# Two layers of linear attention and squared-ReLU feed-forward on one core: the second group's tiles by seven products per pair, M's differences on GpSimd

## The chip, the core and the metric

One core of one Trainium2 chip runs the whole program. The metric is the device time of one execution in microseconds (us), the median of three runs of the same kernel. A profile of one further execution gives the timing of every instruction. Its engines are called as the profile calls them: PE (TensorE matmuls), PEld (TensorE weight loads), DVE (VectorE), ACT (ScalarE), POOL (GpSimd) and SP (the queue that issues the DMAs).

## The reference, cut to what matters

```python
def _A_ref(x, wqkv, wo):                    # S = 2048, D = 640, 32 heads of 20
    q, k, v = split_heads(x @ wqkv)
    phi = lambda t: where(t > 0, t + 1, exp(t)) + 1e-6
    pq, pk = phi(q), phi(k)
    kv = einsum("bhsd,bhse->bhde", pk, v);  z = sum_s(pk)
    o = (pq @ kv) / (pq . z + 1e-6)
    return merge_heads(o) @ wo

def _B_ref(x, w1, b1, w2, b2):              # F = 1728
    h = relu(x @ w1 + b1)
    return (h * h) @ w2 + b2

x = x + A(layernorm(x));  x = x + B(layernorm(x))
x = x + A(layernorm(x));  x = x + B(layernorm(x))
```

Everything is float32. The kernel folds `kv` of all heads and `wo` into one matrix M of 640 x 640, so that the attention's output for a tile of 128 rows is `pT @ M`, where `pT` is the tile's normalized query features, transposed.

## The kernel before, in words

The 2048 rows are 16 tiles of 128 rows, and four groups of four tiles (`TG = 4`). Every float32 operand of a matmul is split in a high part (written by ACT, rounded for TensorE) and a low part (DVE: the value less its high part), and a product is three matmuls, high by low, low by high and high by high (`mm3`, L399 to L403). Matrices M are five row blocks `M[0]` to `M[4]` of 128 rows, each split so.

Each of the two layers has three stages.

**Stage A** (L712 to L841) goes once over the 16 tiles: layer norm, the projections to k and q, their feature maps (`Phi`, L495: `exp` on ACT at L501, then `rest` with DVE's L508 and L509, which empties the PSUM bank), and the sums over rows that M is made of. POOL adds up the key features (`acc`, L697).

**The passage** (L844 to L1052) finishes the q parts that were left over (`late_q`, L847, three PSUM banks in turn from L1043 on: 1, 2, 3), makes M (`kv_make`, `m_make` into the raw rows `m_raw`, L979, L935 to L952; `m_split` writes the split M, L954), and brings the first group's four tiles to the feed-forward stage. For tiles 0 to 3 that is: product with M (`proj`, L424), the residual sum (`b_x1`, L668), the layer norm (`b_norm`, L671: `ln_stats`, L355, with two bn_stats and bn_aggr on DVE and then an add at L362 and a power at L363 on POOL; `ln_apply`, L368, on DVE), and the transposition, by 32 x 32 blocks for tiles 0 and 1 (`blocks_T`, L378, on DVE, then sixteen block moves on ACT, L391) and by TensorE for tiles 2 and 3 (`f_trans`, L1006 and L372). All engines take their instructions in the order in which the program writes them, so `late_q` parts fill PE between these steps. A new `late_q` part may begin in its bank only when L509 has read that bank's earlier part.

**The feed-forward stage** (L1583 to L1615) loops over four groups g and, in each, over 14 blocks c of F. A step is `fc1` (15 matmuls, L1083), `act` (ACT's Relu at L1094, DVE's L1095 to L1097 make the split h), and `fc2` of the block before (15 matmuls, L1132). Between the matmul groups of a step, `run(g, c, place)` calls what a table `events` has for that place: the attention tiles of the **next** group are worked in there. For groups 2 and 3 they go in pairs (`side`, L1491; `Pair`, L1348): two tiles share seven products of half width (320 columns) with sums and differences of row blocks, `p1` to `p7`, of 18 block products together. The needed differences of M's blocks, `ta` and `tb`, are made once per layer by `m_turns` (L1279) on DVE and ACT, out of the split M, at steps 6 to 13 of group 0 (`TURN0`, L67). For group 1 (tiles 4 to 7), worked in during group 0, each tile goes by itself (`single`, L1453): ten half-width block products per tile (two halves of five), at steps 3, 5, 8 and 10 (`OUT0`, L66).

Weights of the feed-forward blocks come through a ring of six buffers by SP (L310). In the first layer two blocks of `w1` and `w2` that stay in memory are loaded raw into the space of `x1` (`raw_stay`, L321, called from L1250) and split in group 0 (`split_stay`, L329).

At the very start PE does `N_WARM` transposes of the identity (L547 to L549) while the first loads are under way.

Of the kernel before, what the change touches and what calls it, by code (L numbers as in the profile page):

```python
# [8 lines left out]
F32 = mybir.dt.float32  # L9
# [29 lines left out]
N_WARM = 25  # L39
# [13 lines left out]
def fast(b):  # L53
    return pair_plan(
        b, (b - 3, 0), (b - 2, 0), [(b - 1, 0), (b - 1, 1), (b - 1, 2), (b - 1, 3)],
        {"p1": (b, 0), "p4": (b, 1), "p6": (b, 2), "p7": (b, 3), "p5": (b, 4),
         "p2": (b + 1, 0), "p3": (b + 1, 2)},
        [((b, "post"), (b + 1, 0), (b + 1, 1), (b + 2, 0), (b + 2, 1), (b + 2, 3)),
         ((b + 1, 3), (b + 1, "post"), (b + 2, 0), (b + 2, 4), (b + 3, 0), (b + 3, 1))],
    )  # L60
# [5 lines left out]
OUT0 = (3, 5, 8, 10)  # L66
TURN0 = (  # L67
    [(6, 2), (7, 2), (7, 3), (8, 1), (8, 2), (8, 3), (8, 4)],
    [(9, 2), (10, 2), (10, 3), (11, 1), (12, 3), (13, 2), (13, 3)],
)  # L70
# [8 lines left out]
def kernel(  # L79
# [50 lines left out]
    def ftile(name):  # L130
        return tmp.tile([P, D], F32, tag="f", name=name, bufs=F_BUFS)
# [223 lines left out]
    def ln_stats(t, xt):  # L355
        st = small.tile([P, 2, 6], F32, tag="bn", name="bn")
        for j in range(2):
            nc.vector.bn_stats(st[:, j], xt[:, j * HD : (j + 1) * HD])
        mv = small.tile([P, 2], F32, tag="mv", name="mv")
        nc.vector.bn_aggr(mv, st)  # L360
        rs = small.tile([P, 1], F32, tag="rs", name="rs")
        nc.gpsimd.tensor_scalar(rs, mv[:, 1:2], LN_EPS, None, op0=ALU.add)  # L362
        nc.gpsimd.tensor_tensor(out=rs, in0=rs, in1=neghalf, op=ALU.pow)  # L363
        sts[t] = mv, rs
# [78 lines left out]
    def a_stats(t):  # L443
        if t < NT:
            ln_stats(("a", t), xt[t])
# [12 lines left out]
    for layer in range(N_LAYERS):  # L458
# [82 lines left out]
        if layer == 0:  # L541
# [11 lines left out]
            a_stats(0)  # L553
# [399 lines left out]

        def m_split(m):  # L954
# [54 lines left out]

        po = {}  # L1010
# [41 lines left out]
        late_rest()  # L1052
        sa.close()
# [200 lines left out]
        def stay(c):  # L1254
# [7 lines left out]

        ta, tb, so = wtile("uT13"), wtile("uT42"), wtile("uS")
        ta, tb, so = (
            ta.rearrange("p (j m n) -> p j m n", j=2, m=2),
            tb.rearrange("p (j m n) -> p j m n", j=2, m=2),
            so.rearrange("p (j n) -> p j n", j=2),
        )  # L1270

        def m_whole(m):
            v = ftile("mf")
            nc.vector.tensor_tensor(
                out=v, in0=M[m][:, 0].bitcast(F32), in1=M[m][:, 1].bitcast(F32), op=ALU.add
            )
            return v

        def m_turns(m):  # L1279

            b1 = m_whole(m)
            yield
            b2 = m_whole(m + 2)
            lo, hi = slice(0, HD), slice(HD, D)
            for i, (out, x, y) in enumerate((
                (b1[:, lo], b1[:, hi], b1[:, lo]),
                (b1[:, hi], b2[:, hi], b1[:, hi]),
                (b2[:, hi], b2[:, hi], b1[:, lo]),
                (b2[:, lo], b2[:, lo], b2[:, hi]),
            )):  # L1290
                if i % 2 == 0:
                    yield
                nc.vector.tensor_tensor(out=out, in0=x, in1=y, op=ALU.subtract)
            yield
            for u, v in ((ta, b1), (tb, b2)):
                nc.scalar.activation(u[:, 0, m], v, AF.Copy)
            for u, v in ((ta, b1), (tb, b2)):
                yield
                nc.vector.tensor_tensor(
                    out=u[:, 1, m], in0=v, in1=u[:, 0, m].bitcast(F32), op=ALU.subtract  # L1300
                )

# [150 lines left out]
        def single(i, b, d, at):  # L1453

            t = TG + i
            if i > 0:
                at(d - 3, "post", lambda: b_load_pq(t))
            at(d - 1, "post", lambda: b_den(t))
            at(d, "post", lambda: b_blocks(t))
            s = d + (i == 0)  # L1460
            at(s, "post", lambda: blocks_move(yzp[t], (0, 1)))
            at(s + 1, "pre", lambda: blocks_move(yzp[t], (2, 3)))
            steps(at, lambda: p_split(t), *[(d + 2, "pre") if i == 0 else (d + 1, "post")] * 2)
            at(b - 3, "post", lambda: b_load_x(t))
            ps = []

            def out():
                yzp.pop(t)
                for j in range(2):
                    s = slice(j * HD, (j + 1) * HD)  # L1470
                    ps.append(fresh(f"po{j}")[:, :HD])
                    for c in range(DC):
                        a = pT[t][:, :, c * P : (c + 1) * P]
                        mm3(ps[j], a[:, 0], a[:, 1], M[c][:, 0, s], M[c][:, 1, s], c == 0, c == DC - 1)
                pT.pop(t)

            def add():
                for j in range(2):
                    v = xr[t][:, j * HD : (j + 1) * HD]
                    nc.vector.tensor_tensor(out=v, in0=ps[j], in1=v, op=ALU.add)  # L1480
                ln_stats(("b", t), xr[t])
                norm(t)

            at(b, "pe", out)
            at(b + 1, "pre", add)
            at(b + 1, "post", lambda: blocks_move(yzx[t], (0, 1)))
            at(b + 1 + 3 * (i == 3), "post", lambda: f_bias(t))
            at(b + 2, "pre", lambda: blocks_move(yzx[t], (2, 3)))
            steps(at, lambda: x_split(t), (b + 2, "post"), (b + 2, "post"))

        def side(g, p, plan, at):  # L1491

            t0, t1 = TG * g + 2 * p, TG * g + 2 * p + 1
            m0, m1, turn, out, back = plan["moves0"], plan["moves1"], plan["turn"], plan["out"], plan["back"]
            for t, (s, pl) in ((t0, m0), (t1, m1)):
# [7 lines left out]
            steps(at, lambda: p_split(t0), (m0[0] + 1, 0), (m0[0] + 1, 2))  # L1503
# [13 lines left out]
            for t, (st, ap_, (s, pl), hi, lo, bi) in ((t1, back[0]), (t0, back[1])):  # L1517
                at(*st, lambda t=t: ln_stats(("b", t), xr[t]))
                at(*ap_, lambda t=t: norm(t))
                for k in range(4):  # L1520
                    at(s + (pl + k) // 5, (pl + k) % 5, lambda t=t, k=k: blocks_move(yzx[t], (k,)))
# [5 lines left out]
        for g in range(NG - 1):  # L1527
# [3 lines left out]
            for p in range(TG // 2):  # L1531
# [5 lines left out]
                if g > 0:  # L1537
                    side(g + 1, p, OUTS[p], at)
            if g == 0:
                for i, b in enumerate(OUT0):  # L1540
                    single(i, b, OUT0[i - 1] if i else 1, at)

                for m in range(2):
                    steps(at, lambda m=m: m_turns(m), *TURN0[m])

# [38 lines left out]
        for g in range(NG):  # L1584
            for c in range(NF):
# [62 lines left out]
```

## Time and profile before

| | |
|---|---|
| time, median of three runs (lowest, highest) | 1345.11 us (1344.97, 1345.32) |
| the profiled execution's own time | 1345.5 us |
| its span, first to last instruction | 1343.4 us |
| what lies around the span | 2.1 us |
| instructions | 19038 |

A row of a group names the line, the engine, the operation, what is written and read, and how often; then the busy time. A row of the timeline is start, duration, engine, line, operation, tiles and count; in brackets stands the idle time of the engine just before, and what ended it. A row of the chain of work that ended last is start, duration, engine and line. A row of a table by stretches has the stretch, its length and each engine's busy time in it.

### The profile page before, as it was taken

To read this page: it belongs to the slowest core of one execution; us is meant where nothing else is said; L and a number is where in the kernel's file an instruction comes from. 1 tells how busy PE (TensorE), PEld (TensorE's weight loads), DVE (VectorE), ACT (ScalarE), POOL (GpSimd) and SP (SyncE) were. 2 spreads that over 40 slices of the span, in tenths; PEclk is the share of its full clock that TensorE was granted. 3 is DMA by queue.
4 is the path that set the end of the run, shared out by engine and by line. 5 is a ranking of instruction groups with operands and counts; after the bars stand their busy time and mean duration, and the time that the engine had idled before them with its cause. 6 is when DMAs were issued, how large, how long until landed. Compare 5 with 4: busy or idle time off the path is not lost.

```text
span 1343.4 us, 19038 instructions
## 1 busy us (share of the span) xinstructions
PE 1337.6 (100%) x6773; PEld 1156.1 (86%) x6773; DVE 924.0 (69%) x1670; ACT 787.3 (59%) x1992; POOL 123.3 (9%) x172
## 2 busy tenths in 40 slices
PE   9999999999999999999999999999999999999998
PEld 8888999988888888888888899998888888888887
DVE  8888868777776776643467678677678667766323
ACT  5888848676547448512647686494746466474120
POOL 2222210000000000000012232100000000000000
PEclk9999999999999999999999999999999999999999
DMA  6787825574645565487521115156546456555635
GB/s 206 255 298 272 286 91 179 197 272 150 245 163 176 201 250 173 156 311 276 221 98 50 49 40 156 41 206 258 178 152 244 167 182 230 196 173 176 248 130 193
DMA packets 85635, 253.43 MB, mean 189 GB/s; under 512 B 11030, under 2 KB 19606, under 8 KB 84902
## 3 DMA queue, kind: packets, MB, share of 16 engines
q1 hardware_dynamic: 85398, 252.04, 53.6%
q8 instruction: 53, 0.87, 0.3%
q14 instruction: 40, 0.33, 0.1%
q10 hardware_dynamic: 144, 0.20, 0.0%
HBM read 193.50 MB, written 56.03 MB: 186 GB/s over the span
## 4 chain that ended last, share of the span: by engine, by line
PE 99%; DMA 0%; ACT 0%; SPq 0%; DVE 0%; DVEq 0%; issue 0%
PE PS L403 38%; PE PS L1132 28%; PE PS L1083 28%; PE PS L424 3%; PE PS L927 1%; PE PS L940 1%; PE PS L736 1%; DMA st<-in_A_wqkv_dram 0%; PE PS L372 0%; PE PS L877 0%; PE PS L1172 0%; ACT kq L189 0%; DVE x L1183 0%; SPq L211 0%; SPq L441 0%; DVEq L1643 0%
## 5 line engine op out<-in xcount | busy, mean ns | idle before, releaser
L391 ACT ACTIVATE z<-y 32x160 f32<-32x160 f32 x1392 | 465.1, 334 | 75.2 <-DVE y L378 59.1
L1083 PE MATMUL PS<-xTb,u 128*128 128x512 f32 x1400 | 333.1, 389 | 0.0
L1083 PEld LDWEIGHTS PS<-xTb,u 128*128 128x128 f32 x1400 | 262.0, 188 | 54.4 <-ACT hr L1094 0.8
L403 PE MATMUL PS<-kq,xT 128*128 128x320 f32 (+2 forms) x1575 | 284.3, 334 | 0.0
L1132 PE MATMUL PS<-u,h 128*128 128x512 f32 x1120 | 276.7, 390 | 0.0
L403 PEld LDWEIGHTS PS<-kq,xT 128*128 128x128 f32 x1575 | 250.3, 188 | 27.3 <-DVE rl L509 1.0
L1132 PEld LDWEIGHTS PS<-u,h 128*128 128x128 f32 x1120 | 208.5, 188 | 40.8
L1094 ACT ACTIVATE hr<-PS,b1sb 128x512 f32<-128x512 f32 x104 | 71.5, 687 | 277.3 <-PE PS L1083 276.4
L1095 DVE TENSOR_TENSOR hr<-hr 128x512 f32<-128x512 f32 x104 | 71.7, 690 | 219.7 <-ACT hr L1094 219.2
L403 PE MATMUL PS<-kh,xh 128*128 128x512 f32 x480 | 124.1, 392 | 0.0
L501 ACT ACTIVATE e<-PS 128x320 f32<-128x320 f32 (+4 forms) x128 | 53.6, 436 | 107.2 <-PE PS L403 98.7
L362 POOL TENSOR_SCALAR rs<-mv 128x1 f32<-128x1 f32 x64 | 28.0, 438 | 865.4 <-DVE mv L360 865.4
L403 PEld LDWEIGHTS PS<-kh,xh 128*128 128x128 f32 x480 | 87.1, 188 | 15.2 <-DVE kh L700 0.4
L508 DVE TENSOR_SCALAR e<-e 128x320 f32<-128x320 f32 (+4 forms) x128 | 41.6, 325 | 69.9 <-ACT e L501 69.4
L1132 PE MATMUL PS<-h,u 128*128 128x512 f32 x280 | 79.0, 390 | 0.0
L1097 DVE TENSOR_TENSOR h<-hr,h 128x512 fp32r<-128x512 f32 x104 | 72.0, 693 | 3.6
L697 POOL TENSOR_TENSOR acc<-acc,r 128x640 f32<-128x640 f32 x30 | 53.8, 1795 | 197.8 <-DVE r L509 197.8
L403 PE MATMUL PS<-uM,pT 128*128 128x320 f32 x408 | 66.2, 309 | 0.0
L403 PEld LDWEIGHTS PS<-uM,pT 128*128 128x128 f32 x408 | 62.3, 188 | 1.9
L1132 PEld LDWEIGHTS PS<-h,u 128*128 128x128 f32 x280 | 52.2, 188 | 10.8 <-DVE h L1108 0.4
L1083 PE MATMUL PS<-xTb,uw 128*128 128x512 f32 x240 | 57.0, 389 | 0.0
L509 DVE SCALAR_TENSOR_TENSOR r<-PS,e 128x512 f32<-128x512 f32 (+2 forms) x104 | 51.1, 492 | 6.1 <-ACT e L501 2.2
(135 smaller groups left out, 1458.5 us busy)
## 6 DMA issues: line engine op xcount, KB each, us to landing
u<-kept_w SPq DMA_DIRECT2D x184, 640.0 KB, 4.2
x<-x SPq DMA_DIRECT2D x48, 320.0 KB, 4.6
kept_w<-uprep SPq DMA_DIRECT2D x23, 640.0 KB, 4.6
pqt<-pq SPq DMA_DIRECT2D x32, 320.0 KB, 4.9
x<-xr SPq DMA_DIRECT2D x32, 320.0 KB, 3.8
st<-in_B_w_dram SPq DMA_DIRECT2D x22, 320.0 KB, 6.2
pq<-r SPq DMA_DIRECT2D x20, 320.0 KB
kept_kq<-kq SPq DMA_DIRECT2D x10, 640.0 KB, 6.2
```

Source lines behind the costliest of these rows:

```text
L391: nc.scalar.activation(d, v, AF.Copy)
L403: nc.tensor.matmul(ps, a, b, start=first and i == 0, stop=last and i == 2)
L424: nc.tensor.matmul(ps[:, j * 512 : j * 512 + HD], aT[:, k, c, :], w[c][:, l, j * HD : (j + 1) * HD], start=c == 0 and i == 0, stop=c == DC ...
L501: nc.scalar.activation(self.e[:, a:b], ps, AF.Exp)
L508: nc.vector.tensor_scalar(e, e, 1.0, PHI_EPS, op0=ALU.min, op1=ALU.add)
L509: nc.vector.scalar_tensor_tensor(out=self.r[:, a:b], in0=ps, scalar=0.0, in1=e, op0=ALU.max, op1=ALU.add)
L697: nc.gpsimd.tensor_tensor(out=acc, in0=acc, in1=r, op=ALU.add)
L1083: nc.tensor.matmul(ps, a[:, d, :], bb[:, d, :], start=n == 0, stop=n == len(order) - 1)
L1094: nc.scalar.activation(r, ps, AF.Relu, bias=b1sb[:, c : c + 1])
L1095: nc.vector.tensor_tensor(out=r, in0=r, in1=r, op=ALU.mult)
L1097: nc.vector.tensor_tensor(out=h[:, 1], in0=r, in1=h[:, 0].bitcast(F32), op=ALU.subtract)
L1132: nc.tensor.matmul(ps, l, r, start=first and k == 0, stop=last and k == len(a) - 1)
```

## The change

- `OUT0` becomes two pair plans. Group 1's four tiles go through `side` and `Pair` like those of groups 2 and 3, at steps 5 and 10 of group 0, the second pair with its block moves at steps 5 and 8 and one of its four groups of moves on DVE. `single`, `TURN0`, `m_whole` and `m_turns` go.
- `ta` and `tb` are made in the passage. `m_sums` takes the differences in place on the raw rows `m_raw` with POOL, four subtractions of half a row block for each of two m; `b_norm` issues two of them each time, behind `ln_stats` and ahead of `ln_apply`; what is left would come at the end (`m_sum(9)`). Then four splits (ACT and DVE) stand at the end of the passage, behind the last `late_rest` and ahead of the release of that stage's memory.
- In the pair plans, the high and low parts of the first tile's `x_split`, its `f_bias` and the low part of its `p_split` are put at other places.
- `split_stay` is called once at step 0 of group 0 in place of three times.
- 22 warm-up transposes in place of 25; the very first layer norm's epsilon is added by DVE in place of POOL.

```diff
-N_WARM = 25
+N_WARM = 22
-def fast(b):
+def fast(b, m0=None, m1=None):
     return pair_plan(
-        b, (b - 3, 0), (b - 2, 0), ...
+        b, m0 or (b - 3, 0), m1 or (b - 2, 0), ...
-         ((b + 1, 3), (b + 1, "post"), (b + 2, 0), (b + 2, 4), (b + 3, 0), (b + 3, 1))],
+         ((b + 1, 3), (b + 1, "post"), (b + 2, 0), (b + 2, "post"), (b + 3, "pre"), (b + 3, 4))],
-OUT0 = (3, 5, 8, 10)
-TURN0 = (
...
+OUT0 = (fast(5), {**fast(10, (5, 0), (8, 0)), "vec": ((0, 2),)})
+STAY = 1

-    def ln_stats(t, xt):
+    def ln_stats(t, xt, add=nc.gpsimd):
...
-        nc.gpsimd.tensor_scalar(rs, mv[:, 1:2], LN_EPS, None, op0=ALU.add)
+        add.tensor_scalar(rs, mv[:, 1:2], LN_EPS, None, op0=ALU.add)
         nc.gpsimd.tensor_tensor(out=rs, in0=rs, in1=neghalf, op=ALU.pow)
-            a_stats(0)
+            a_stats(0, add=nc.vector)

         def b_norm(t):
             ln_stats(("b", t), xr[t])
+            m_sum(2)
             xn[t] = ftile("xn")
             ln_apply(("b", t), xn[t], xr[t])

+        def m_sums(m):
+            b1, b2, lo, hi = m_raw[m], m_raw[m + 2], slice(0, HD), slice(HD, D)
+            for out, x, y in (
+                (b1[:, lo], b1[:, hi], b1[:, lo]),
+                (b1[:, hi], b2[:, hi], b1[:, hi]),
+                (b2[:, hi], b2[:, hi], b1[:, lo]),
+                (b2[:, lo], b2[:, lo], b2[:, hi]),
+            ):
+                nc.gpsimd.tensor_tensor(out=out, in0=x, in1=y, op=ALU.subtract)
+                yield
+        m_fill.extend(m_sums(m) for m in range(2))
...
         late_rest()
+        ta, tb, so = wtile("uT13"), wtile("uT42"), wtile("uS")
...
+        m_sum(9)
+        for u, v in ((ta, 0), (tb, 2)):
+            for m in range(2):
+                split(u[:, 0, m], u[:, 1, m], m_raw[m + v])
         sa.close()
...
-        def m_whole(m):
...
-        def m_turns(m):
...
-        def single(i, b, d, at):
...
-            steps(at, lambda: p_split(t0), (m0[0] + 1, 0), (m0[0] + 1, 2))
+            steps(at, lambda: p_split(t0), (m0[0] + 1, 0), (m0[0] + 1, 4))
...
-                    for _ in range(3 if c == 0 else 1):
+                    for _ in range(STAY if c == 0 else 1):
                         wu.split_stay()
```

More of the change, by code (lines that the diff above doesn't have):

```diff
@@ L1260, in stay @@
                 n_stage += 1
[L1265 to L1270, printed above, removed]
-        def m_whole(m):
[L1273 to L1277, printed above, removed]
-        def m_turns(m):
[L1281 to L1301, printed above, removed]
         def s_turns(t):
@@ L1451, in norm @@
             yzx[t] = blocks_T(xn.pop(t))
-        def single(i, b, d, at):
[L1455 to L1489, printed above, removed]
         def side(g, p, plan, at):
@@ L1535, in at @@
                     events.setdefault((*divmod(n, NF), place), []).append(f)
[L1537 to L1544, printed above, removed]
+                side(g + 1, p, OUTS[p] if g > 0 else OUT0[p], at)
         def run(g, c, place):
```

25 lines of the change are left out of this document (18 added, 7 removed).

## The prediction

> **What bounds the kernel now.** I read the page first: which engine is full, and who ends the chain of work.
>
> ```profile
> PE 1337.6 (100%) x6773; PEld 1156.1 (86%) x6773; DVE 924.0 (69%) x1670; ACT 787.3 (59%) x1992; POOL 123.3 (9%) x172
> PE 99%; DMA 0%; ACT 0%; SPq 0%; DVE 0%; DVEq 0%; issue 0%
> ```
>
> PE never waits, so only two things move the time: matmuls taken out or put in, and waits that a change opens in PE's stream. Second, the chain in order of time, for the price of matmuls and for the passage of layer 0:
>
> ```profile
> 242.99 4.41 PE PS L403 x30
> 247.40 0.55 PE PS L372 x5
> 247.95 2.20 PE PS L403 x15
> 250.15 0.55 PE PS L372 x5
> 250.69 2.30 PE PS L403 x15
> 253.00 6.83 PE PS L1083 x30
> ...
> 276.82 4.39 PE PS L403 x30
> ...
> 379.77 1.32 PE PS L403 x9
> ```
>
> The row at 276.82 is a `single` tile's product; that at 379.77 is p4 of a pair. 4.39 / 30 and 1.32 / 9 both give 0.147 us for a half-width matmul. The first six rows are PE's end of the passage: two `late_q` parts (I call them B and C), the transposes of tile 2, a part D, the transposes of tile 3, a part E, then `fc1`. Third, the timeline of DVE, ACT, POOL and PEld there, since they feed PE:
>
> ```profile
> 233.25 0.61 DVE L368 TENSOR_SCALAR xn<-xr,mv,rs 128x640 f32<-128x640 f32 x1 [1.00 <-POOL rs L363]
> 233.90 0.84 DVE L378 STREAM_TRANSPOSE y<-xn 128x640 f32<-128x640 f32 x1
> ...
> 234.78 5.54 ACT L391 ACTIVATE z<-y 32x160 f32<-32x160 f32 x16
> ...
> 241.12 0.82 DVE L137 TENSOR_TENSOR xTb<-z,xTb 128x640 fp32r<-128x640 f32 x1 [1.18 <-ACT xTb L136]
> 241.86 0.82 DVE L668 TENSOR_TENSOR xr<-PS,xr 128x640 f32<-128x640 f32 x1
> 244.24 0.57 POOL L363 TENSOR_TENSOR rs<-rs,scalars 128x1 f32<-128x1 f32 x1
> 244.84 0.61 DVE L368 TENSOR_SCALAR xn<-xr,mv,rs 128x640 f32<-128x640 f32 x1 [1.00 <-POOL rs L363]
> 245.37 0.32 DVE L508 TENSOR_SCALAR e<-e 128x320 f32<-128x320 f32 x1
> 245.72 0.49 DVE L509 SCALAR_TENSOR_TENSOR rl<-PS,e 128x320 f32<-128x320 f32 x1
> 248.20 0.22 POOL L362 TENSOR_SCALAR rs<-mv 128x1 f32<-128x1 f32 x1 [3.39 <-DVE mv L360]
> 249.11 0.61 DVE L368 TENSOR_SCALAR xn<-xr,mv,rs 128x640 f32<-128x640 f32 x1 [1.00 <-POOL rs L363]
> 249.64 0.32 DVE L508 TENSOR_SCALAR e<-e 128x320 f32<-128x320 f32 x1
> 249.84 0.62 PEld L372 LDWEIGHTS PS<-ident,xn 128*128 128x128 f32 x5
> 249.99 0.49 DVE L509 SCALAR_TENSOR_TENSOR rl<-PS,e 128x320 f32<-128x320 f32 x1
> 250.53 2.20 PEld L403 LDWEIGHTS PS<-kq,xT 128*128 128x128 f32 x15
> 254.47 0.49 DVE L509 SCALAR_TENSOR_TENSOR rl<-PS,e 128x320 f32<-128x320 f32 x1
> ```
>
> This is one unbroken chain behind a full PE. Tile 0's apply (233.25) lets the block moves go (234.78, right behind 233.90 + 0.84), these end tile 0's split (241.12, for which DVE waited), and from there DVE goes tile 2's sum, statistics and apply (244.84), part A's L508 and L509, tile 3's sum and apply (249.11), part B's L508 and L509. It meets PE twice without slack: tile 3's apply ends at 249.72 and its weight load is at 249.84; B's L509 ends at 250.48 and E, in the same bank, loads at 250.53. What makes DVE later here by d makes PE later by d, less about 0.1.
>
> **Part by part.** *Products.* A tile by itself has 30 matmuls, a pair 54: 6 fewer per pair, two pairs per layer, two layers: 24 x 0.147 = **3.5 us less**, straight off PE. This is sure where the pairs' preparation keeps up. Its cover, from a stretch of group 1 with two pairs (us, then busy PE, PEld, DVE, ACT):
>
> ```profile
> 429.00:484.00 55.00, 55.00 (x263) 46.80 (x262) 40.84 (x73) 33.85 (x90) 1.58 (x4) 1.00 0.66 236
> ```
>
> PE is full with DVE at 74%. Group 0 has less of the old work (no tile sums, no strip), but up to 0.82 of f_bias and 0.82 of a unit's low part in each of steps 0 to 3. ACT's worst is step 3: 16 moves in 5.54, a Relu 0.69, two high parts of 0.74: 7.7 against 6.8 of PE; the step before has 7.0, the one after is light. h is needed 6.8 after its `fc1` and made in 2.6 (256.46 to 259.06, rows further down), so a lag of up to 4.2 is covered. The moved places in the pair plans (x_split, f_bias, p_split) stay in steps with as much room; I cost them at nothing, covered by that same 4.2; without it each is at most its own 0.8.
>
> *POOL's differences.* Eight of 128x320 per layer, two behind each layer norm's power. L697's add of 128x640, alone, takes 1.62 (below). Half of that is 0.81; with L362's 0.22 for one element as a fixed part it is 0.92. I take 0.87. On POOL itself they hide: each pair ends 1.7 after the power, and L362 idles 3.39 or more before each later tile. The question is DVE. What DVE and POOL do to each other:
>
> ```profile
> 21.55 1.03 POOL L695 COPY acc<-r 128x640 f32<-128x640 f32 x1 [0.56 <-DVE r L509]
> 21.96 0.80 DVE L508 TENSOR_SCALAR e<-e 128x320 f32<-128x320 f32 x1
> ...
> 106.64 1.62 POOL L697 TENSOR_TENSOR acc<-acc,r 128x640 f32<-128x640 f32 x1 [8.64 <-DVE r L509]
> ...
> 106.86 0.56 DVE L509 SCALAR_TENSOR_TENSOR r<-PS,e 128x384 f32<-128x384 f32 x1
> 107.34 1.61 DVE L137 TENSOR_TENSOR xh<-xt,xh 128x640 fp32r<-128x640 f32 x1
> ...
> 13.15 1.00 POOL L363 TENSOR_TENSOR rs<-rs,scalars 128x1 f32<-128x1 f32 x1
> 14.11 0.20 POOL L588 MEMSET mask<- 120x120 f32 x1
> ```
>
> L508 takes 0.80 in place of 0.32 and ends 0.18 after the copy; L137 takes 1.61 in place of 0.82 and ends 0.69 after the add. Both stood until POOL was done. L509, with one input in PSUM, isn't touched. So the apply (L368, SBUF to SBUF like L508) and L508 stand while a difference runs, and the differences are issued at just the moment when L368 is released. A POOL instruction that needs nothing starts 0.04 before its forerunner's end (14.11 against 14.15); L368 starts 0.03 after the power's end (244.81). By 0.07 POOL is first. The rule in the Trainium skill, SBUF — State Buffer, section Who interferes with whom, is the same and speaks against this change: a one-input VectorE copy or scalar operation within SBUF and a GpSimd instruction exclude each other, and the second to issue is blocked until the first has finished; the rows at 21.55 and 21.96 agree.
>
> With POOL first, counted from the power's end: the first difference ends at 0.83, L368 at about 1.30 in place of 0.64: 0.65 late. The second difference has waited longest and goes next, to 1.96; L508, 0.32 long, ends at 2.17 in place of 0.89: 1.28 late. Along the chain: tile 0 gives 0.65 (the transposition L378 isn't held), tile 2 with A's L508 1.28, tile 3 with B's L508 1.28. Tile 1 gives nothing: DVE idles 1.18 behind it. Sum 3.2 per layer at part E (0.65 + 1.28 + 0.65 at the transposes of tile 3, the rest at E), **6.4 us more** for two. With DVE first, tile 0 gives nothing and each L508 is 0.62 late: 1.24 per layer, 2.5 in all. For a wait that the trace doesn't show, nothing is the other bound. I take 6.4, because the only row of an unhindered POOL successor has it first.
>
> *Four splits at the passage's end.* ACT is free after its last exp, at 253.5, and its four copies of 0.74 (0.65 apart) end with the Relu's release. DVE's four low parts of 0.82, 0.73 apart, follow 254.47:
>
> ```profile
> 256.46 0.69 ACT L1094 ACTIVATE hr<-PS,b1sb 128x512 f32<-128x512 f32 x1 [2.99 <-PE PS L1083]
> 257.18 0.69 DVE L1095 TENSOR_TENSOR hr<-hr 128x512 f32<-128x512 f32 x1 [2.22 <-ACT hr L1094]
> ...
> 258.37 0.69 DVE L1097 TENSOR_TENSOR h<-hr,h 128x512 fp32r<-128x512 f32 x1
> ...
> 259.44 2.68 PEld L1132 LDWEIGHTS PS<-u,h 128*128 128x128 f32 x12
> ```
>
> They end near 257.8, so L1095 to L1097 come 0.6 later, h's low part at 259.7; the second weight load needs it at 259.7 to 259.9. I count nothing, at most 0.2 per layer. In layer 0 the release of M's raw rows comes 3 us later, and SP's raw loads into `x1`, with a ring load, an xr and a pq load behind them, can wait for it; their first split then comes at 262.4 in place of 259.5 and the second Relu behind it on ACT at 263.1, while its h is due at 266.6. Covered by that room.
>
> *Removed on DVE and ACT:* `m_turns`, two of three early unit splits: not on PE's path, nothing. *The start:* the epsilon on DVE saves at most the 0.4 between the aggregate's end and the power; but
>
> ```profile
> 7.07 0.74 ACT L189 ACTIVATE kq<-st 128x640 fp32r<-128x640 f32 x1 [1.64 <-DMA st<-in_A_wqkv_dram]
> 7.71 0.75 ACT L569 ACTIVATE xT<-PS 128x256 fp32r<-128x256 f32 x2
> ```
>
> the first tile's copy stands behind a weight load's landing, and PE starts behind that. Three warm-ups fewer end 0.7 earlier, ahead of the same wait. Nothing; 0.2 either way.
>
> **Sum.** 3.5 less, 6.4 more: 2.9 more than the profiled execution's 1345.5 (span 1343.4, and 2.1 around it), which stood 0.4 above the median of 1345.1. So **1348.0 us**.
>
> **Rivals.** *DVE first* (27%): 0.07 is little, and the differences for tiles 0 and 2 have loads and splits of their rows to wait for, if only in form. 3.5 less, 2.5 more: 1344.1, not slower. It decides at the power's end: whichever engine's instruction starts first. *No collision that PE feels* (12%): the waits fall in slack that I don't see: 1341.6, faster. For it speaks that PE's ends are modelled; against it the 0.05 at part E. *Pairs late in group 0* (8%): the pairs' products stand in PE's stream at steps 5 and 10; if ACT's moves lag by one group of four (1.38) for each of four pairs, 5.5 on top of either case, 1350 to 1353; then the seven products save nothing. *Mixed order* (5%): POOL first for some tiles: 1345 to 1347.
>
> **Numbers.** My forecast has 48%, with its own range of 1346.8 to 1349.4 (differences of 0.81 to 0.92, and 0.2 per layer at h). The range of 1342.8 to 1349.5 holds this, *DVE first* down to the case in which only one of its two waits is felt, and *mixed*; *no collision* and the top of *pairs late* are outside. A measurement tells about 0.2%, 2.7 us, from no change: under 1342.4 lies *no collision*, 13% with the edges; above 1347.8 lie some three fifths of my case and *pairs late*, 37%; between them 50%.
>
> **What would show it.** After the change: L368 of the passage at about 1.3 in place of 0.61 and a POOL L363 followed within 0.1 by a subtraction (POOL first), or L368 as before and L508 lengthened (DVE first); a wait of PE for tile 3's xn and for L509 ahead of E, 3.2 or 1.2 together per layer; eight subtractions of about 0.87; 54 products' matmuls at steps 5 and 10 with no wait of PE there; `fc1` starting in layer 0 at about 256.2. Wrong would be: POOL's subtraction not holding L368, or PE waiting in group 0.

## The result, and the profile after

| | before | after |
|---|---|---|
| time, median of six runs (lowest, highest) | 1345.21 us (1344.97, 1346.15) | 1352.08 us (1350.93, 1353.88) |
| after / before, 95% interval | | 1.0052 (1.0039 to 1.0064) |
| profiled execution: time; span | 1345.5; 1343.4 | 1351.43; 1349.7 |

The change makes the kernel slower by 0.5%. The forecast was +2.9 us; the profiled span grew by 6.3, the median by 6.9. To see where, take instructions that both traces have and subtract their start times. This table does so for the changed kernel and, further on, for experiments (each against the kernel before; all in us; the landmarks are rows of the timeline, the Relus counted from the layer's start).

| landmark | before | after | e1 | e4 | e5 | e13 | e14 |
|---|---|---|---|---|---|---|---|
| stage A, layer 0: first exp | 14.03 | -0.48 | -0.73 | +0.17 | -0.33 | -0.96 | -0.45 |
| layer 0, group 0: first Relu | 256.46 | +4.04 | -0.67 | +3.24 | +0.80 | -0.35 | +0.17 |
| layer 0, group 1: Relu of block 2 | 379.37 | +3.85 | -0.96 | +3.18 | +0.59 | +0.38 | -0.93 |
| layer 1: first exp | 679.07 | +3.83 | -0.97 | +3.15 | +0.59 | +0.34 | -0.88 |
| layer 1, group 0: first Relu | 920.77 | +6.85 | -0.92 | +7.75 | +1.66 | +0.90 | -0.32 |
| layer 1, group 1: Relu of block 8 | 1090.80 | +6.27 | -1.47 | +7.77 | +1.06 | +0.36 | -2.18 |
| end | 1343.44 | +6.27 | -1.46 | +7.78 | +1.05 | +0.39 | -2.18 |

Read it by differences down a column. The stretch from the first exp to the first Relu holds stage A and the passage: +4.52 in layer 0 (-0.48 to +4.04) and +3.02 in layer 1 (+3.83 to +6.85). From there to group 1 lie the pairs of group 0: -0.19 and -0.58, where -1.76 each was forecast. Everywhere else the two kernels keep step.

The passage of layer 0, timeline of the changed kernel, the rows that answer to those shown of before (its lines are three lower: L365 is the apply, L505 and L506 empty the `late_q` bank, L964 is POOL's subtraction):

```profile
244.30 0.57 POOL L360 TENSOR_TENSOR rs<-rs,scalars 128x1 f32<-128x1 f32 x1
244.84 1.96 POOL L964 TENSOR_TENSOR Mr<-Mr 128x320 f32<-128x320 f32 x2
...
244.91 1.16 DVE L365 TENSOR_SCALAR xn<-xr,mv,rs 128x640 f32<-128x640 f32 x1 [1.00 <-POOL rs L360]
245.99 1.00 DVE L505 TENSOR_SCALAR e<-e 128x320 f32<-128x320 f32 x1
247.02 0.49 DVE L506 SCALAR_TENSOR_TENSOR rl<-PS,e 128x320 f32<-128x320 f32 x1
...
250.33 1.93 POOL L964 TENSOR_TENSOR Mr<-Mr 128x320 f32<-128x320 f32 x2
...
250.40 1.14 DVE L365 TENSOR_SCALAR xn<-xr,mv,rs 128x640 f32<-128x640 f32 x1 [1.00 <-POOL rs L360]
251.46 0.98 DVE L505 TENSOR_SCALAR e<-e 128x320 f32<-128x320 f32 x1
...
251.59 0.77 PE L369 MATMUL PS<-ident,xn 128*128 128x128 f32 x5 [1.39 <-DVE xn L365]
253.03 3.84 PE L400 MATMUL PS<-kq,xT 128*128 128x320 f32 x15 [0.67 <-DVE rl L506]
```

POOL's first subtraction starts 0.03 before the power's end (244.87), the apply 0.07 after POOL: the apply takes 1.16 in place of 0.61, L505 1.00 in place of 0.32, the plain L506 its usual 0.49. PE, which never waited here, now waits 1.39 for tile 3 and 0.67 ahead of part E. That is the forecast mechanism. What the forecast doesn't have is the last row: part E takes 3.84 in place of 2.30. The stretches of that table, with the granted clock behind the five busy times:

```profile
249.00:252.00 3.00, 1.61 (x13) 1.34 (x12) 1.97 (x4) 0.72 (x2) 2.35 (x4) 1.00 0.06 24
253.00:257.00 4.00, 3.98 (x16) 3.97 (x17) 3.62 (x7) 0.20 (x2) 0.00 (x0) 0.59 0.21 82
```

Behind the waits the TensorE clock is at 0.59 of full speed; the trace's clock record has 0.50 from 253.7 on for 3.41 us, and 1.00 before and after. And all waits of PE in the changed kernel (us in total, times, longest):

```profile
PE PS L369 <- DVE xn L365: 2.8, 2, 1.4
...
PE PS L400 <- DVE rl L506: 1.3, 2, 0.7
PE PS L1120 <- DVE hr L1140: 0.9, 2, 0.4
...
PE PS L400 <- DVE xr L665: 0.6, 2, 0.3
...
PE PS L400 <- DVE xr L1380: 0.2, 1, 0.2
```

The first, second and fourth are the passage, twice. The third and fifth stand in group 0, where the forecast has none. These two make 1.1 together, less than the 2.8 by which the products fall short of their 3.5; the ends of PE's matmuls are modelled, and the weight loads of the same places wait longer: 1.7 for L1140, 1.0 for the strip, and 0.6 for L1380, this last in layer 0 alone.

### The profile page after: what moved, and what is told of

Same layout as the page of the kernel before. It is cut to its first block, busy times and chain, and to the rows that moved or that the text cites. A ratio compares the mean times of both kernels' runs of the same rounds, so it can differ in the third digit from the quotient of the medians.

```text
span 1349.7 us, 19057 instructions
## 1 busy us (share of the span) xinstructions
PE 1337.4 (99%) x6746; PEld 1152.3 (85%) x6746; DVE 942.0 (70%) x1703; ACT 788.3 (58%) x1996; POOL 138.8 (10%) x187
## 4 chain that ended last, share of the span: by engine, by line
PE 90%; DVE 6%; ACT 1%; DMA 1%; issue 1%; POOL 0%; SPq 0%; DVEq 0%; POOLq 0%
PE PS L400 36%; PE PS L1120 26%; PE PS L1169 25%; PE PS L421 1%; PE PS L925 1%; PE PS L938 1%; ACT z L388 1%; PE PS L734 1%; DVE y L375 1%; DMA pqt<-pq 1%; DVE xn L365 1%; DVE bn L355 1%; DVE x L1220 0%; DVE xr L665 0%; DMA st<-in_A_wqkv_dram 0%
## 5 line engine op out<-in xcount | busy, mean ns | idle before, releaser
L388 ACT ACTIVATE z<-y 32x160 f32<-32x160 f32 x1384 | 462.3, 334 | 63.0 <-DVE y L375 46.9
L505 DVE TENSOR_SCALAR e<-e 128x320 f32<-128x320 f32 (+4 forms) x128 | 44.2, 345 | 70.9 <-ACT e L498 70.6
L506 DVE SCALAR_TENSOR_TENSOR r<-PS,e 128x512 f32<-128x512 f32 (+2 forms) x104 | 51.1, 492 | 5.8 <-ACT e L498 2.4
L1120 PEld LDWEIGHTS PS<-xTb,uw 128*128 128x128 f32 x240 | 45.1, 188 | 9.4
L1133 DVE CAST h<-hr 128x512 fp32r<-128x512 f32 x104 | 44.4, 427 | 7.4
```

The costliest lines, as they stand in the source:

```text
L388: nc.scalar.activation(d, v, AF.Copy)
L505: nc.vector.tensor_scalar(e, e, 1.0, PHI_EPS, op0=ALU.min, op1=ALU.add)
L506: nc.vector.scalar_tensor_tensor(out=self.r[:, a:b], in0=ps, scalar=0.0, in1=e, op0=ALU.max, op1=ALU.add)
L1120: nc.tensor.matmul(ps, a[:, d, :], bb[:, d, :], start=n == 0, stop=n == len(order) - 1)
L1133: nc.vector.tensor_copy(h[:, 0], r)
```

## The experiments

**e1: without the subtractions.**

```diff
             for out, x, y in (
...
-                nc.gpsimd.tensor_tensor(out=out, in0=x, in1=y, op=ALU.subtract)
                 yield
```

> The changed kernel without the eight POOL subtractions per layer (the splits take M's raw rows, so the pairs' products are not the reference's). Theory, that the subtractions hold DVE in the passage and with it PE: the waits of PE for tile 3's xn and for L506 ahead of part E go, about 2.9 us per layer, and with them the 1.5 to 1.7 us of half clock in layer 0: span 1342.2, time about 1344, that is 0.1% under before. Rival, that the four splits at the passage's end or the later release of the raw rows hold PE: span stays near 1349.7. In both, some 1.1 to 1.3 us per layer lost in group 0 stay.

Measured: 1344.57 us, ratio 0.9998 (0.9989 to 1.0007), span 1342.0. The stretch up to the first Relu costs 0.06 and 0.05 in place of 4.52 and 3.02 (table). The four splits at the passage's end, the later raw loads and the shortened start are all still in it, so none of them is the cause of this part. The rows of e1 that answer to part E and its clock:

```profile
249.81 2.47 PE L400 MATMUL PS<-kq,xT 128*128 128x320 f32 x15
```

```profile
253.00:257.00 4.00, 4.00 (x19) 3.29 (x19) 3.97 (x7) 2.95 (x5) 0.00 (x0) 1.00 0.21 82
```

But the pairs of group 0 still give only 0.29 and 0.55 (-0.67 to -0.96, -0.92 to -1.47). That loss has another cause than the subtractions.

**e4: the subtractions alone**, put into the kernel before at the same place, with nobody using their results.

> The kernel before with the POOL subtractions added at the changed kernel's place, their results unused. Theory: they alone cost 2.9 us per layer in the passage, plus 1.7 us for each layer in which the clock is then halved: span 1349.2 to 1352.6. Rival, that the cost in the passage needs the splits or the pairs: span 1343.4 to 1344.

Measured: 1353.4 us, ratio 1.0062 (1.0047 to 1.0077), span 1351.2. Alone they cost 7.8 of span: +3.07 (0.17 to 3.24) in layer 0 and +4.60 (3.15 to 7.75) in layer 1, where this time the clock falls (0.50 from 921.04 on, for 3.41):

```profile
919.61 0.77 PE L372 MATMUL PS<-ident,xn 128*128 128x128 f32 x5 [1.41 <-DVE xn L368]
921.04 4.01 PE L403 MATMUL PS<-kq,xT 128*128 128x320 f32 x15 [0.67 <-DVE rl L509]
```

A passage without the fallen clock costs 3.07 here and 3.02 in the changed kernel. So the forecast of 3.2 per layer for the waits stands, and the half clock is 1.5 more (4.60 and 4.52 against these), in one layer or the other.

**e2: a short instruction of POOL between the power and the subtractions**, to let DVE in first.

```diff
             ln_stats(("b", t), xr[t])
+            nc.gpsimd.memset(gap, 0.0)
             m_sum(2)
```

> The changed kernel with one POOL memset of a 128x128 scratch tile (about 0.2 us) between the power and the two subtractions. Theory, that the order at the power's end decides: L365 is first again, 0.61 in place of 1.16, L505 stays long (about 1.0); the stall is about 1.3 us per layer in place of 2.9 and the clock keeps full: span about 1344.7. Rival, that a subtraction holds DVE whichever comes first, or that the memset holds it too: L365 at 1.2 or more, span 1349 to 1351.

Measured: 1353.23 us, ratio 1.0064 (1.0047 to 1.008). DVE was not let in:

```profile
233.09 0.20 POOL L671 MEMSET gap<- 128x128 f32 x1
233.25 1.98 POOL L966 TENSOR_TENSOR Mr<-Mr 128x320 f32<-128x320 f32 x2
```

```profile
233.18 1.31 DVE L366 TENSOR_SCALAR xn<-xr,mv,rs 128x640 f32<-128x640 f32 x1 [1.00 <-POOL rs L361]
```

The apply stood during the memset and, though it had waited since 233.18, during the first subtraction as well; it ends at 234.48, 0.35 behind that one (234.14). That the engine that waits goes next, as the prediction has it, fits what happens between the two subtractions (the second begins at 234.22, and only after it has begun does the apply end), but not what happens behind the memset. The subtraction began 0.04 before the memset's end (233.29), as it begins before the power's end in the changed kernel; whether that lead decides here too, no run tests. A memset of 0.20 as a gap is no cure.

**e5: the same subtractions on DVE**, in the time in which it waits for POOL's add and power.

```diff
-                nc.gpsimd.tensor_tensor(out=out, in0=x, in1=y, op=ALU.subtract)
+                nc.vector.tensor_tensor(out=out, in0=x, in1=y, op=ALU.subtract)
```

> The changed kernel with the eight subtractions on DVE in place of POOL, at the same place in the program: DVE waits 1.0 us there for POOL's add and power, and two subtractions take 2 x 0.49. Theory, that only the simultaneous work of POOL and DVE costs: they fill DVE's wait, but POOL's add and power, small as they are, now stand behind them (the power took 1.0 in place of 0.57 beside a two-input DVE step at the start); about 0.3 to 0.6 late per tile on the chain of tiles 0, 2 and 3: 0.9 to 1.8 us per layer, span 1343.8 to 1345.6. Rival, that the wait hides them wholly: span 1342.0 as without subtractions. Other rival, that DVE's time is what lacks: 2.9 per layer as with POOL, span 1348.

Measured: 1346.7 us, ratio 1.0011 (1.0001 to 1.002); 5.4 us better than the changed kernel; the span, 1344.5, is inside the expected 1343.8 to 1345.6.

```profile
248.42 0.96 DVE L964 TENSOR_TENSOR Mr<-Mr 128x320 f32<-128x320 f32 x2
249.84 0.61 DVE L365 TENSOR_SCALAR xn<-xr,mv,rs 128x640 f32<-128x640 f32 x1 [0.46 <-POOL rs L360]
```

```profile
248.59 0.35 POOL L359 TENSOR_SCALAR rs<-mv 128x1 f32<-128x1 f32 x1 [3.40 <-DVE mv L357]
249.02 0.79 POOL L360 TENSOR_TENSOR rs<-rs,scalars 128x1 f32<-128x1 f32 x1
```

Now it is POOL that stands: its add takes 0.35 in place of 0.22 and its power 0.79 in place of 0.57. Together that makes the apply some 0.35 late, not 0.55 and more, and nothing queues behind it. PE's weight loads wait 0.6 per layer for tile 3 (1.7 in e4), and the clock stays at 1.0.

**e6: PE kept busy in its waits**, to test the clock by itself: 12 transposes into a free bank ahead of tile 3's, 5 behind.

```diff
+        fill(12)
         f_trans(3, bank(4, 2))
+        fill(5)
         late_q(9, False)
```

> The changed kernel with 12 transposes of the identity on PE ahead of tile 3's transposes and 5 behind them (about 1.3 and 0.55 us of work that nobody reads, into PE's idle time of 1.4 and 0.7 us). Theory, that the idle PE in the passage brings the half clock: the granted clock stays 1.00 from first to last, part E takes 2.3 to 2.5 in place of 3.84, and nothing else moves: span 1348.1 or less, 1.5 us under the changed kernel's profile, and no run with a clock below 1.000. Rival, that the half clock has another cause: the clock record and E stay as they are, span 1349.5 to 1350.5.

Measured: 1351.47 us, ratio 1.0046 (1.0031 to 1.0061). Stretches of e6 with the passages of layers 0 and 1, the clock third from the end:

```profile
5.00:9.00 4.00, 2.73 (x15) 1.91 (x14) 2.51 (x7) 2.27 (x5) 0.55 (x1) 1.00 0.93 321
9.00:13.00 4.00, 4.00 (x18) 4.00 (x18) 3.96 (x8) 2.98 (x5) 0.46 (x1) 0.57 1.03 403
250.00:258.00 8.00, 7.77 (x56) 7.22 (x55) 6.86 (x12) 2.85 (x6) 2.61 (x4) 1.00 0.21 82
918.00:926.00 8.00, 7.78 (x55) 7.13 (x54) 6.86 (x13) 2.90 (x6) 2.63 (x4) 1.00 0.21 79
```

With PE busy the clock stays up in both passages, and part E takes 2.47 and 2.46. The passages cost 3.08 and 3.02 by the landmarks: the waits alone. In this execution the clock fell at the start instead (9.1 to 12.5), where the first weight landed late and PE idled; that is why its own profiled time, 1352.63, is no better. The median is 0.6 below the changed kernel's, and with four executions between 1350.6 and 1352.6 it can't size the drop; the passages of the trace do.

**e3: the start alone**: the kernel before with 22 warm-ups and the epsilon on DVE.

> The kernel before with 22 warm-ups and the first epsilon on DVE, nothing else. If the 0.48 us by which the changed kernel is ahead after the start comes from these: span 1342.9, time 0.5 us under before, first half-width matmul at 7.6 in place of 8.1. Rival, the prediction's: PE starts when a weight load lands, so nothing, span 1343.4.

Measured: 1344.88 us, ratio 0.9997 (0.9988 to 1.0007): no difference that a measurement tells. The chain at the start shows why. In the changed kernel it goes through the landing of a weight, in e3 through the warm-ups:

```profile
1.70 4.79 DMA st<-in_A_wqkv_dram
...
7.58 1.46 PE PS L734 x7
```

```profile
1.42 4.96 PE PS L547 x22
...
7.29 1.75 PE PS L736 x9
```

The landing (6.49 here) comes at 5.8 to 7.2 in the profiled executions, and the first product at 7.2 to 8.3. In the profiled kernel before, the copy behind the landing began at 7.07 and the first product at 8.13. The 0.5 of the first landmark is this spread, and the fewer warm-ups count only where the landing is early.

**e7: the pairs in group 0, first guess.** DVE's L1140, which reads the single bank of `fc1` at block 13, stands behind a bias addition (L677, 0.83); e7 puts both of the second pair's to a later step.

```diff
-OUT0 = (fast(5), {**fast(10, (5, 0), (8, 0)), "vec": ((0, 2),)})
+SECOND = fast(10, (5, 0), (8, 0))
+SECOND["back"] = [(*b[:5], (16, "post")) for b in SECOND["back"]]
+OUT0 = (fast(5), {**SECOND, "vec": ((0, 2),)})
```

> The changed kernel with both f_bias steps of group 0's second pair put behind step 2 of group 1 (from steps 12 and 13). Theory, that DVE's backlog at the end of group 0 holds PE by way of the bank that L1140 reads and of the strip's bank: the waits of PE for L1140 (0.9 per layer) and for the strip (0.5) shrink to under 0.4 together, about 1.0 us per layer less. The passage stays as it is, half clock included: span about 1347.7. Rival, that the loss there comes from ACT's moves or the ring loads: both waits stay, span 1349.7.

Measured: 1352.63 us, ratio 1.0052 (1.0035 to 1.0069), with the half clock in both layers of the profiled execution. The wait for L1140 (here L1142) is unchanged, 1.7 at the weight loads. The guess was wrong: the bias only filled a gap in which DVE waits for ACT.

```profile
362.02 1.04 DVE L388 COPY z<-y 32x160 f32<-32x160 f32 x4
363.93 0.83 DVE L1344 TENSOR_TENSOR xTb<-z,xTb 128x640 fp32r<-128x640 f32 x1 [0.86 <-ACT xTb L1342]
364.67 0.68 DVE L1142 TENSOR_TENSOR hr<-PS,hr 64x512 f32<-64x512 f32 x1
```

The order is: DVE's copies (L388), ACT's high part of x, DVE's low part, L1142. The copies are late.

**e8, e10, e11: the subtractions behind the apply, and a surprise.** POOL first copies one column of `xn`, so that it waits for the apply, and subtracts then.

```diff
             ln_stats(("b", t), xr[t])
-            m_sum(2)
             xn[t] = ftile("xn")
             ln_apply(("b", t), xn[t], xr[t])
+            if t < 3:
+                nc.gpsimd.tensor_copy(seen, xn[t][:, :1])
+                m_sum(2 if t else 4)
```

> The changed kernel with the subtractions behind the apply: POOL first copies one column of xn, which makes it wait for L365, and then does four subtractions behind tile 0, two behind tiles 1 and 2, none behind tile 3. Theory, that only what DVE does at the same moment counts: behind tile 2 the subtractions run beside L506, L665 and the statistics, which have at most one input in SBUF, and hold at most L505 by 1; behind tile 0 they hold one split on DVE, which has 1.2 us of room. L365 is 0.61 again; passage stall 0 to 0.7 us per layer, full clock: span 1342.0 to 1343.4. Rival, that POOL's subtractions slow the passage wherever they are: 2 us or more per layer, span over 1346.

Measured: 1356.59 us, ratio 1.0086 (1.0071 to 1.0101). The collision is gone (part E takes 2.47 with no wait of PE ahead of it; one wait of 0.3 for the residual sum L665, here L666, stays in each passage), and yet the kernel is the slowest so far. Against before, the feed-forward stage of layer 0 drifts by 3.1 us between the Relus of block 2 of group 1 and of block 9 of group 3, where nothing was changed and PE waits for nothing. The groups of PE in the stretch 480 to 600, e8 first and then the kernel before (mean ns of one behind the busy time):

```profile
L1172 PE MATMUL PS<-u,h 128*128 128x512 f32 x153 | 39.5, 394 | 0.0
```

```profile
L1132 PE MATMUL PS<-u,h 128*128 128x512 f32 x163 | 41.0, 390 | 0.0
```

The same matmul takes 394 ns in place of 390. e8 has one new buffer, `seen`, of one float per partition. By the expectation of e11 the working buffers behind it lie 32 bytes further in the compiled kernel; no trace holds an address, so that step isn't shown. e11 tests the declaration alone: the kernel before with the buffer declared and never used. e10 is e8 with the buffer 64 bytes wide.

> The kernel before with one unused tile of one float per partition declared ahead of the working buffers: in the compiled kernel all of these lie 32 bytes further, nothing else changes. Theory (matmuls read more slowly from the shifted buffers): about 1% over stage A's and the feed-forward's matmuls, 1352 to 1358, fc2's matmuls at 394 ns, no new wait. Rival (the drift had to do with GpSimd's new order): 1345.2, within 0.1% of the kernel before.

Measured: 1357.01 us, ratio 1.0092 (1.0078 to 1.0106), fc2's matmuls at 394. The unused buffer costs 12 us by itself.

> As the run in which GpSimd subtracts only behind the apply (it first copies one column of xn), but the column that it copies to is 16 floats wide in place of one, so that every later buffer lies 64 bytes further than in the changed kernel in place of 32. In that earlier run no wait of PE had grown, yet the feed-forward stage had drifted by 1.15% (3.1 us in the 270 us from the first step of group 1 to the last of group 3), with fc2's matmuls at 394 ns in place of 390. Theory: the 32 bytes cost that, not the subtractions. Then the drift is gone, fc2's matmuls take 390 ns again, and the time is that of the kernel without subtractions, 1344.6 (1343.8 to 1345.6). Rival: the subtractions behind the apply, or GpSimd's copy of a column, cost it in a way that the waits don't show: 1352 or more, with the drift.

Measured: 1352.67 us, ratio 1.0058 (1.0046 to 1.0071): the rival's number, but not its reason. fc2's matmuls take 392, and the drift over the same stretch is 1.97 in place of e11's 3.14. A buffer of 64 bytes per partition is not harmless either; in e2, whose new buffer has 512, there is no drift (+3.20 to +3.18) and 390 again. That the subtractions behind the apply don't cause the drift is shown by e13, further on, which has them and no drift.

**e12a, e12b: the second pair a step earlier**, on top of e10 (and so with its buffer).

```diff
-OUT0 = (fast(5), {**fast(10, (5, 0), (8, 0)), "vec": ((0, 2),)})
+OUT0 = (fast(5), {**fast(9, (5, 0), (7, 0)), "vec": ((0, 2),)})
```

> As the run with the 64 bytes, and the second pair of group 0 one step earlier (products at step 9 in place of 10, its second block moves at step 7 in place of 8; the copies on DVE stay). Theory: PE's waits at step 13 (for hr, 0.45 per layer) and behind it (strip 0.5, hr 0.27) come from that pair's last preparation, the high and low parts of x, which stand in ACT's and DVE's order ahead of the act of block 13; a step earlier they are done before it, and 0.8 to 1.2 per layer comes back: 1342 to 1343.5. Rival: ACT has no room in steps 6 to 9 for two pairs' moves (5.5 a tile and step beside a Relu, against 6.8 of PE), and the waits turn up there: 1344.5 or more.

> As the run with the second pair a step earlier, and all of its block moves on ACT (no copies on DVE). Theory (DVE's chain sets the late steps, ACT has room): 0 to 0.5 below that run. Rival (ACT sets them): four more moves, 1.4 per layer, show as a wait of PE at one of the steps 6 to 12, 0.5 to 2.8 above that run.

Measured: 1363.24 us, ratio 1.0139 (1.0125 to 1.0152), and 1364.0 us, 1.014 (1.0125 to 1.0156): the rival of e12a in full, 10.6 and 11.3 above e10. The two lie 0.8 apart, and their executions overlap (1362.5 to 1365.3, 1363.3 to 1365.8), so e12b decides nothing. With two pairs' moves in the same steps ACT is late by more than a group of moves, and in each layer the clock falls to 0.50 for 3.41 near the end of the wait (from 325.71 and 998.14); e12a's largest waits:

```profile
PEld PS L1123 <- ACT hr L1134: 10.0, 2, 5.0
```

**e13: the subtractions behind the apply, nothing moved.** As e8, but the column goes beside two constants that already have a buffer.

```diff
-    scalars = cpool.tile([P, 2], F32, name="scalars")
+    scalars = cpool.tile([P, 3], F32, name="scalars")
...
+                nc.gpsimd.tensor_copy(scalars[:, 2:3], xn[t][:, :1])
+                m_sum(2 if t else 4)
```

> GpSimd's subtractions behind the apply (it first copies one column of xn), with the target column put beside two constants that already have a buffer, so that no other buffer moves against the changed kernel. Theory (the earlier two such runs were slow by their moved buffers alone): fc2's matmuls take 390 ns, no drift over groups 1 to 3, no wait for tile 3's xn and no PE at half clock in the passage; the time is that of the kernel without the subtractions, 1344.6 (1343.8 to 1345.4), some 7.5 below the changed kernel. Rival (the order itself costs it): 1350 or more, with the drift or a wait in the passage.

Measured: 1345.53 us, ratio 1.0001 (0.9992 to 1.001): 6.6 below the changed kernel, 0.1 above the range of the expectation, with fc2 at 390 and the clock at 1.0. By order alone the collision is gone:

```profile
248.69 0.61 DVE L365 TENSOR_SCALAR xn<-xr,mv,rs 128x640 f32<-128x640 f32 x1 [0.99 <-POOL rs L360]
249.22 0.32 DVE L505 TENSOR_SCALAR e<-e 128x320 f32<-128x320 f32 x1
```

0.6 per layer stays in the passage (-0.96 to -0.35, +0.34 to +0.90). Half of it is one wait of PE, 0.30 at 242.32 in layer 0, for the residual sum L665. DVE is late there because the collision has moved to two other instructions, the split of tile 0 and the subtractions behind tile 1; in e1 the same split takes 0.83:

```profile
239.01 1.84 POOL L966 TENSOR_TENSOR Mr<-Mr 128x320 f32<-128x320 f32 x2
240.15 1.38 DVE L134 TENSOR_TENSOR xTb<-z,xTb 128x640 fp32r<-128x640 f32 x1 [0.46 <-ACT xTb L133]
```

In group 0 the waits at block 13 stand as in the changed kernel. The pairs give 0.54 in layer 1, but in layer 0 they cost 0.73 (-0.35 to +0.38): the wait for `xr` at step 5 has grown to 0.8 of PE. DVE works there without a gap over 0.1 from 282.54 to the sum that PE waits for (L1382, 293.04), and begins late, behind ACT's high part of a raw unit, which ACT does after a tile's block moves:

```profile
282.54 0.83 DVE L251 TENSOR_TENSOR uw<-x,uw 128x640 fp32r<-128x640 f32 x1 [0.78 <-ACT uw L247]
```

Only layer 0 has such units, and only layer 0 has this wait; no run takes them away.

**e14: e13, and DVE's lag at step 12 of group 0 taken away.** Ahead of the late copies DVE works on a denominator for the next group (L626 to L638) and its block transposition (L375), 3.8 in all, which nobody needs yet. e14 does them a step earlier, for the first pair of groups 2 and 3.

```diff
-OUTS = ({**fast(2), ("den", 1): ((-1, 1), (-1, 3))}, fast(9))
+OUTS = ({**fast(2), ("den", 0): ((-4, "post"), (-3, "post")), ("den", 1): ((-1, 1), (-1, 3))}, fast(9))
```

> As the run before it, and for the first pair of each later group the first tile's denominator goes from steps 11 (behind) and 12 to step 10 (behind) and 11 (behind): 3.9 of DVE's work that stood ahead of its copies for the second pair of group 0 at step 12. Theory: PE's waits at step 13 (hr 0.45 at PE, 0.7 at its weight load, then strip 0.4) come from DVE's lag there; the copies then come about 2 earlier, ACT has the high part of x done before the Relu of block 13, and 0.5 to 1.1 per layer comes back: 1342.3 to 1343.6. Rival (ACT's own 5.5 of moves per tile sets it): the same waits, within 0.4 of the run before it; or, if DVE's sums at steps 10 and 11 wait behind the denominator instead, slower by up to 2.

Measured: **1343.16 us, ratio 0.9983 (0.9975 to 0.9992)**, better than both kernels, inside the expected 1342.3 to 1343.6, and 2.4 below e13. The end of group 0, first in the changed kernel (DVE and ACT, then PE's weight loads), then in e14:

```profile
360.41 0.84 DVE L375 STREAM_TRANSPOSE y<-pqt 128x640 f32<-128x640 f32 x1
361.27 1.05 DVE L386 COPY z<-y 32x160 f32<-32x160 f32 x4
...
362.41 0.74 ACT L1340 ACTIVATE xTb<-z 128x640 fp32r<-128x640 f32 x1 [1.36 <-DVE z L386]
363.19 0.82 DVE L1342 TENSOR_TENSOR xTb<-z,xTb 128x640 fp32r<-128x640 f32 x1
363.93 0.68 DVE L1140 TENSOR_TENSOR hr<-PS,hr 64x512 f32<-64x512 f32 x1
```

```profile
358.16 2.23 PEld L1120 LDWEIGHTS PS<-xTb,u 128*128 128x128 f32 x10
...
364.66 3.31 PEld L1120 LDWEIGHTS PS<-xTb,u 128*128 128x128 f32 x15 [0.87 <-DVE hr L1140]
...
376.86 0.53 PEld L1169 LDWEIGHTS PS<-h,u 128*128 128x128 f32 x3 [0.50 <-DVE strip L1185]
```

```profile
356.18 1.04 DVE L386 COPY z<-y 32x160 f32<-32x160 f32 x4
...
359.14 0.68 DVE L1142 TENSOR_TENSOR hr<-PS,hr 64x512 f32<-64x512 f32 x1
```

```profile
354.71 2.23 PEld L1122 LDWEIGHTS PS<-xTb,u 128*128 128x128 f32 x10
...
360.37 3.36 PEld L1122 LDWEIGHTS PS<-xTb,u 128*128 128x128 f32 x15
```

Counted from the weight load of block 13's `fc1` (358.16; 354.71), the copies start 3.1 behind it in the changed kernel, where ACT waits 1.36 for them, and 1.5 in e14. The read of the bank ends at 364.61 in the one, where the next `fc1` has waited 0.87 for it, and 0.55 ahead of that `fc1` in the other (359.82, 360.37). No wait for hr or strip is left in e14's list. By the landmarks the pairs now give 1.10 in layer 0 and 1.86 in layer 1; in e13 they cost 0.73 and gave 0.54. So the moved work brought 1.8 and 1.3, more than the 0.5 to 1.1 per layer that was expected.

## Why the prediction was wrong

The forecast of 1348.0 us (range to 1349.5) is 4.1 below the measured median and 3.4 below the profiled execution. Its collision in the passage came as forecast. What failed is the cover of the seven products in group 0 (2.8 us), and a term is missing, the clock (1.5 us). Point by point:

- **POOL's subtractions hold the apply and L508, POOL first: right.** Per layer 3.2 was forecast; the runs show 3.0 in layer 1 of the changed kernel, 3.07 in e4 and 3.08 and 3.02 in e6. The steps agree one by one. Counted from the power's end (244.87), the first subtraction ends at 0.85 (forecast 0.83), the apply at 1.20 (1.30), the second subtraction at 1.93 (1.96) and L505 at 2.12 (2.17); the first subtraction takes 0.88, the second 1.01, where 0.87 was taken. Choosing POOL first by a lead of 0.07 was right: 0.07 is what the rows at 244.84 and 244.91 show. The rival *DVE first* does not occur: each of the eight applies in the passages of after, of e4, of e6 and of e7 takes 1.14 to 1.17.
- **What a wait does to PE: missing.** The sum counted a wait at its own length. Two waits of 1.4 and 0.7 close together can also halve the clock for 3.41 us, which costs 1.5; with PE kept busy in them it stays at 1.00 (e6). The Trainium skill, TensorE: Matmul & The Clock Gate, Part 1, has a window of 3413 ns that runs free of the program, and half speed after an idle one. The length agrees with the record's 3.41, and a free-running window agrees with where the drop falls: in the same passages, behind like waits, in layer 0 alone (after), in layer 1 alone (e2, e4) or in both (e7). But PE was not idle for a whole window: of the 3.41 before 253.7 it worked 1.4. So here less than a whole idle window was enough. The mean granted clock of the changed kernel's six runs lies between 0.997 and 1.000, and one drop makes 0.0013 of the span, so by this estimate they had none to two drops each. That doesn't explain their whole spread of 2.9 us (before: 1.2): the slowest, 1353.88, has 0.999.
- **Seven products, 3.5 us less: the count right, its cover wrong.** This is the step that failed most: 0.77 came (0.19 and 0.58), 2.8 too little. The prediction put the preparation's effect on PE in group 0 at nothing, "covered by that same 4.2", and took the 4.2 from how long h may lag behind its Relu. At block 13 h is not what is due first: L1140 must read the bank before the next `fc1` may write it, and that `fc1`'s weight load waited 0.87 for it. The rival *pairs late in group 0* had 8%, and named ACT's moves. At the end of group 0 the runs show DVE: ACT waits 1.36 for its copies, and these stand behind work for the next group. e14, which moves that work, gives 1.86 in layer 1, the forecast 1.76 within 0.1, and 1.10 in layer 0, where one wait at step 5 (0.6 of PE for `xr`) is left. For that one the rival may be right in part: in e13 the chain before it goes back to ACT's moves and a raw unit's split. This is read from a trace and not tested.
- **ACT is close to full: right as a reading, wrong in its use.** The forecast put ACT's worst step at 7.7 against 6.8. e12a shows what that means: one step less room and PE waits 4.6 per layer.
- **Splits at the passage's end, raw loads, work that DVE and ACT no longer have: nothing, right as far as the first Relu** (e1: 0.06 and 0.05 with all of them in). Whether the raw units have a part in the wait at step 5 of layer 0 is open.
- **The start: nothing, right within its spread** (e3); the profiled pair of executions differs by 0.5 because a weight landed 0.6 earlier.

So the sum, by what the traces show for the profiled span: -0.5 start, +6.0 waits, +1.5 clock, -0.8 products, 6.2 of the measured 6.3. The forecast had 0, +6.4, 0 and -3.5. The median lies 0.65 above the profiled execution; that part the sum doesn't cover.

Open: the other half of the 0.6 per layer that stays in the passage in e13 and e14; the wait at step 5 of layer 0; and why a memset of POOL doesn't hand DVE the turn.

## What to carry to other kernels

Before moving work to an idle engine, look at what the other engine starts at the very instant at which that work is released: here the same eight subtractions per layer cost 7.8 us ahead of the apply (e4, 1.5 of it the clock) and 1.2 behind it (e13, both passages). Price a wait of a full PE at more than its length when waits of some 2 us in all fall within 3.4: here it was 1.5 more, in some passages and not in others. And when a saving is "covered by slack", name for each moved step the buffer that ends the slack; a single bank can take it to nothing, and then even the unneeded work of the next group, standing earlier in an engine's order, decides.

## What the runs showed of the hardware that was not expected

- **One more buffer, never used, changes the speed of matmuls.** With 4 bytes per partition declared ahead of the working buffers, fc2's 128x512 matmuls take 394 ns in place of 390 (`fc1`'s 390 in place of 389) and the kernel 12 us more (e11), with no new wait and the clock at 1.0; with 64 bytes fc2's take 392 (e10), with 512 bytes 390 (e2). That the shifted places of the buffers do it is the likely reading, but the traces hold no addresses. Any experiment that adds a buffer should be read with that in mind.
- **POOL's next instruction can pass a waiting DVE**: behind a memset of 0.20 the apply, ready since 233.18, still stood until the subtraction that began at 233.25 was done (e2).
- **It works the other way round too**: with the subtractions on DVE, POOL's one-column power takes 0.79 in place of 0.57 (e5).
